# One kernel, the same operations, a new order of issue

## The chip, the core and the metric

The kernel runs on one core of a Trainium2 chip. The metric is the device time of one execution in microseconds (us). The core has five engines with a queue each: PE (matrix products; "PEld" in the profile is its weight load), DVE (element-wise work), ACT (activations and copies out of PSUM), POOL (small element-wise work, accumulating DMAs) and SP (here it only issues DMAs). An engine takes its instructions in the order in which the program lists them; it waits at the head of its queue until the semaphores of that instruction are set, and all that stands behind waits with it. 16 DMA engines carry the transfers that SP, ACT and POOL issue.

## The reference

Two blocks follow each other. The first is attention with a polynomial sketch as its kernel: for 4 batches, 4 heads, 1088 positions and 32 channels,

```python
def phi(x):
    a = np.einsum('rd,bhsd->bhsr', S1, x)
    b = np.einsum('rd,bhsd->bhsr', S2, x)
    return np.einsum('bhsi,bhsj->bhsij', a, b).reshape(*x.shape[:-1], r * r)
q_p, k_p = (phi(q), phi(k))
kv = np.einsum('bhsf,bhsd->bhfd', k_p, v)
z = np.sum(k_p, axis=2)
num = np.einsum('bhsf,bhfd->bhsd', q_p, kv)
den = np.einsum('bhsf,bhf->bhs', q_p, z)[..., None] + 1e-06
```

and its result is num / den. The heads are then joined to x of 4 x 1088 x 128, and the second block mixes along the positions:

```python
theta = x @ w_theta
zr, zi = x * np.cos(theta), x * np.sin(theta)
y = np.einsum('ts,bsd->btd', w_tok_r, zr) + np.einsum('ts,bsd->btd', w_tok_i, zi)
u = x + y
out = u + np.maximum(u @ w_ch, 0.0)
```

The two mixing matrices are 1088 x 1088 of 64-bit floats; they are most of what is read (17 blocks of 128 x 1088 words of 8 bytes, 1088 KB each), and their product with the z values is most of the arithmetic.

## The kernel before

**Operations.** The body never issues anything directly. It calls op(engine, duration, function, writes, reads, ...) some 1020 times, and each call makes a numbered operation (0 to 1019), of one to some forty instructions of one engine: "P" for PE, "V" for DVE, "A" for ACT, "G" for POOL, "S" for SP. The number counts the calls in the order of the program text.

**Order.** At the end, Layout.run takes the operations in the order that the tuple ORDER lists, and Layout.issue emits them. STARTS holds a start in hundredths of a microsecond for each place of ORDER, from a search that was run beforehand. These starts are used for two things only: which buffer of a class an operation's tile gets (a slot that is free at that start), and how many idle matmuls (`fill`, line 428) are put into gaps of PE. The durations given to op, and lk, are inputs of that search; what is emitted does not read lk, and durations enter only through those two uses.

**What the operations do, in rough order.**

- Loads. k, q and v of each batch are 576 KB each (line 671, line 668 for k of batches 0 and 1, which ACT issues). k of batches 1 to 3 is loaded twice; the second copy (line 714, "kh") is the target of an accumulating DMA that POOL issues (line 393, `big<-hf`). q of batch 3 comes in blocks turned on the way: four operations (37 to 40) of four DMAs each, line 663, 36 KB in runs of 128 bytes. The row blocks of the two matrices are "row 0" to "row 16" (line 642, `zs<-w_tok`).
- Each row block is converted from 64-bit words: two ACT operations (lines 643 and 645) into two `big` buffers, then two DVE operations. The raw block sits in one of five `zs` buffers, and the buffer is free again after the two ACT operations.
- Attention for batch 0, then 1, 2 and 3: sums over the keys ("sums", "rest"), features of k ("kT", "kf", "kv"), the chain of small scale factors ("chain"), q slices ("qT", "q0"), "levels", "den", "num", then "theta".
- Mixing. For batch 0 and batch 1 all 17 row blocks are multiplied with z and summed in PSUM ("mix"); batches 2 and 3 share seven half-size products in Winograd's scheme ("m1" to "m7"). All these matmuls are at line 399. "out" adds x, multiplies by w_ch and stores (line 1299).

**Transfers and their semaphores.** The framework gives every transfer that SP or ACT issues one of eight completion semaphores, in turn. A transfer that reuses a semaphore waits, at the head of the issuing queue, until the transfer eight places before it has landed.

**What the change touches.** ORDER and STARTS (lines 34 on), and one line of `finish` (line 1325), which gives the search a smaller duration and lk for one store operation.

## Time and profile before

| | us |
|---|---|
| median of three timed runs | 217.78 |
| these runs | 218.26, 217.74, 217.78 |
| the profiled execution, its own time | 217.81 |
| its span, first to last instruction | 215.9 |
| around the span | 1.9 |

The profile page is of that one execution. It gives each engine's busy time, the span cut in 40 slices of 5.4 us, the DMA queues, the chain of work that ended last, and the costliest groups of instructions. Views of the same trace give busy times in chosen stretches, the waits, and the instructions of one queue in order of time. PE's records are pipelined: a matmul's record is longer than the time from it to the next one, so that a busy PE shows no gap where the next matmul comes only a little late.

### The profile page before, as it was taken

What the parts mean: (1) busy time and instruction counts of PE and PEld (TensorE: products, weight loads), DVE (VectorE), ACT (ScalarE), POOL (GpSimd) and SP (SyncE); (2) the same over time, 40 slices, a digit from 0 to 9 for tenths busy, and PEclk for the clock granted to TensorE, in tenths of its full rate; (3) what the DMA queues carried; (4) which work ended last, traced back from release to release, by engine and by line L of the source; (5) the groups of instructions that cost most, each with busy time, mean ns of one, the idle gap of its engine ahead of it and who ended that gap; (6) DMA issues with size and microseconds to landing.
All of it is one profiled execution on the core that took longest, in us unless ns stands there. A gap on an engine that the chain in (4) does not pass through costs nothing.

```text
span 215.9 us, 5832 instructions
## 1 busy us (share of the span) xinstructions
PE 208.9 (97%) x2396; PEld 152.8 (71%) x2396; DVE 174.3 (81%) x343; ACT 114.5 (53%) x256; POOL 59.7 (28%) x105
## 2 busy tenths in 40 slices
PE   7899999999999999999999999999999999999992
PEld 7677798868866666866668666667677776666781
DVE  1799998999999998999999798885994747456263
ACT  4899989999998895798704233363810000000000
POOL 1272740306400000604004100000006489950403
PEclk9999999999999999999999999999999999999998
DMA  6999999995998993192002402424050420010735
GB/s 222 395 418 419 384 365 420 425 315 97 360 285 267 416 432 145 75 308 45 0 0 32 74 3 112 114 109 112 2 88 15 67 39 0 0 23 8 125 55 103
DMA packets 28046, 37.09 MB, mean 172 GB/s; under 512 B 20564, under 2 KB 23044, under 8 KB 25844
## 3 DMA queue, kind: packets, MB, share of 16 engines
q1 hardware_dynamic: 22868, 31.86, 42.4%
q0 software_dynamic: 1552, 3.25, 7.2%
q10 hardware_dynamic: 3600, 1.62, 2.8%
q8 instruction: 19, 0.31, 0.6%
q14 instruction: 7, 0.06, 0.1%
HBM read 29.84 MB, written 4.00 MB: 157 GB/s over the span
## 4 chain that ended last, share of the span: by engine, by line
PE 63%; DMA 18%; ACT 14%; issue 2%; SPq 1%; DVE 1%; POOL 1%; POOLq 0%; ACTq 0%
PE ps L399 61%; DMA zs<-w_tok 13%; DMA big<-k_l 5%; ACT big L645 4%; ACT big L643 3%; ACT lv L1056 1%; PE ps L1131 1%; ACT big L1021 1%; ACT g L1199 1%; ACT g L1202 1%; ACT g L1205 1%; ACT g L1203 1%; POOL out L1299 1%; SPq L671 0%; ACT g L1135 0%
## 5 line engine op out<-in xcount | busy, mean ns | idle before, releaser
L399 PE MATMUL ps<-big,zs 128*128 128x384 f32 (+2 forms) x380 | 110.5, 436 | 0.0
L399 PEld LDWEIGHTS ps<-big,zs 128*128 128x128 f32 x380 | 66.9, 190 | 32.5
L379 POOL TENSOR_TENSOR big<-big,big 128x544 f32<-128x544 f32 x16 | 22.1, 1458 | 48.6 <-DVE big L379 44.6
L399 PE MATMUL ps<-big,big 128*32 128x32 f32 (+2 forms) x352 | 22.8, 234 | 0.0
L643 ACT ACTIVATE big<-zs 128x1088 f32<-128x1088 f32 x17 | 20.9, 1231 | 1.5 <-DMA zs<-w_tok 0.9
L379 DVE CUSTOM_DVE_ANT_0 big<-big,big 128x2176 uint16<-128x2176 uint16 x17 | 21.5, 1275 | 0.0
L645 ACT ACTIVATE big<-zs 128x1088 int32<-128x1088 uint32 (+1 forms) x18 | 21.4, 1194 | 0.3 <-DMA zs<-w_tok 0.3
L1338 ACT COPY big<-ps 80x256 f32<-80x256 f32 x1 | 0.4, 368 | 39.6 <-DMA out<-g 39.6
L399 PEld LDWEIGHTS ps<-big,big 128*32 128x32 f32 (+1 forms) x352 | 15.3, 124 | 6.8 <-issue 0.8
L1276 ACT COPY g<-ps 128x384 f32<-128x384 f32 (+1 forms) x6 | 2.5, 466 | 23.4 <-PE ps L399 23.4
L379 DVE TENSOR_TENSOR big<-big 128x544 f32<-128x544 f32 x8 | 9.5, 1204 | 5.6 <-PE ps L399 5.6
L383 DVE TENSOR_SCALAR big<-big 128x1088 int32<-128x1088 int32 x17 | 12.2, 719 | 0.0
L379 POOL TENSOR_TENSOR mf<-mv,sm 128x32 f32<-128x32 f16 (+1 forms) x3 | 0.8, 262 | 39.1 <-DVE sm L379 39.1
L428 PE MATMUL ps<-idle 128*128 128x112 bf16 (+1 forms) x67 | 10.0, 312 | 1.3 <-POOL idle L430 1.3
L379 DVE TENSOR_TENSOR g<-lv 128x768 f32<-128x768 f32 x12 | 11.1, 950 | 0.1
L399 PEld LDWEIGHTS ps<-w,big 128*128 128x128 f32 (+1 forms) x76 | 9.8, 189 | 1.4
L379 DVE TENSOR_TENSOR big<-big,hf 128x1152 f32<-128x1152 f32 x8 | 10.7, 1351 | 0.0
L399 PE MATMUL ps<-w,big 128*128 128x128 f32 (+1 forms) x76 | 10.5, 278 | 0.0
L399 PE MATMUL ps<-sbk,g 128*128 128x64 f32 x72 | 10.0, 276 | 0.3 <-ACT g L793 0.3
L379 DVE TENSOR_TENSOR zs<-zs,g 128x384 f32<-128x384 f32 (+2 forms) x24 | 9.8, 447 | 0.2
L386 DVE SCALAR_TENSOR_TENSOR big<-ps,even,big 128x384 f32<-128x384 f32 (+1 forms) x10 | 4.8, 493 | 6.3 <-PE ps L399 6.2
L1199 ACT ACTIVATE g<-ps 128x384 f32<-128x384 f32 x12 | 5.9, 504 | 7.3 <-PE ps L399 7.3
(199 smaller groups left out, 379.2 us busy)
## 6 DMA issues: line engine op xcount, KB each, us to landing
zs<-w_tok SPq DMA_DIRECT2D x17, 1088.0 KB, 10.6
big<-k_l SPq DMA_DIRECT2D x5, 576.0 KB, 13.2
big<-v_l SPq DMA_DIRECT2D x4, 576.0 KB, 15.6
big<-q_l SPq DMA_DIRECT2D x3, 576.0 KB, 10.7
big<-hf POOLq DMA_DIRECT2D x3, 576.0 KB, 10.0
far<-zs SPq DMA_DIRECT2D x3, 576.0 KB, 2.8
zs<-far SPq DMA_DIRECT2D x12, 144.0 KB, 4.3
big<-k_l ACTq DMA_DIRECT2D x2, 576.0 KB, 4.4
```

Of the source, the lines that this page charges most:

```text
L379: eng.tensor_tensor(out=o, in0=a, in1=b, op=f)
L383: (eng or V).tensor_scalar(out=o, in0=a, scalar1=s1, scalar2=s2, op0=op0, **kw)
L386: (eng or V).scalar_tensor_tensor(out=o, in0=a, scalar=s, in1=b, op0=op0, op1=op1)
L399: T.matmul(o, lhs, rhs, start=start, stop=stop, skip_group_check=True)
L428: T.matmul(nowhere()[:, :n], idle()[:, 0:P], idle()[:, :n], start=True, stop=True, skip_group_check=True)
L643: op("A", 0.22 + n * 0.0009, lambda: A.activation(dfn(), words_of(raw(), n)[1].bitcast(F32), AF.Prelu, scale=2.0**-112, alpha=-(2.0**32)), ...
L645: op("A", 0.22 + n * 0.0009, lambda: A.activation(stp(), words_of(raw(), n)[0].bitcast(U32), AF.Copy, scale=2.0**-29), [stp], [raw])
L1021: op("A", act(GW) + 0.1, lambda g=g, tr=tr: A.activation(f()[:, g * GW:(g + 1) * GW], tr(), AF.Copy, scale=s()[:, 0:1]), [(f, g)], [tr, (s ...
L1056: op("A", act(480), lambda g=g, lp=lp: A.copy(lv().rearrange("p l (c n) -> p l c n", n=HR)[:, :, g * GC:(g + 1) * GC], lp().rearrange("p c ...
L1131: T.transpose(tr()[:, i * P:(i + 1) * P], qp()[:, i * H + 2 * n:i * H + 2 * n + 2].rearrange("p h i j -> p (h i j)"), ident())
L1199: op("A", act(GW), lambda cs=cs, th=th: A.activation(cs()[:, 0], th(), AF.Copy, bias=ROUND), [(cs, 0)], [th])
L1276: op("A", act(w), lambda: A.copy(u(), yp()[:, :w]), [uT], [yp])
```

## The change

The operations and their code are the same. ORDER lists them in another order, and STARTS has other starts. Of the 412 PE operations 47 keep their place in PE's queue, of DVE's 266 also 47, of ACT's 237 it is 45, of POOL's 53 it is 23 and of SP's 52 it is 16. The idle matmuls of 384 columns go from 28 to 26. The order of the transfers, up to the last row block, is as follows (k2 is k of batch 2, kh its second copy, q3a to q3d the four operations 40, 38, 37 and 39; the ACT queue issues k0 and k1):

```
before: k0 k1 k3 q0 row1 k2 w2 q2 row3 kh1 v0 row8 q1 row2 v1 row0 v3 kh3 row7 row5 row4 kh2
        q3d q3c row6 v2 row9 q3a q3b row10 row13 row11 row15 row14 row12 row16
after:  k0 k1 k3 row1 k2 q0 w2 row3 q2 q1 kh1 v0 row2 row0 v2 q3a q3b v3 v1 kh3 row7 row6 row4
        kh2 row9 row5 row8 q3c q3d row12 row10 row11 row13 row14 row15 row16
```

In the last 20 places of ORDER no engine's own order changes. The one line of code:

```diff
@@ finish, line 1325
         elif b and t0 < 2 * GW:
-            op("S", w * P * 4 / 100e3, lambda: (store(SY, 0, 2), store(G, 2, 4)), [], [ot], due, lk=4)
+            op("S", w * P * 2 / 100e3, lambda: (store(SY, 0, 2), store(G, 2, 4)), [], [ot], due, lk=2)
```

and the tables, cut to their first line each:

```diff
 ORDER = (
-    29, 32, 4, 2, 5, 0, 1, 3, 34, 30, 356, 50, 33, 102, 44, 96, 6, 108, 103, 36, 7, 51, 366, 54, 144, 8, 97, 10, 9,
...
+    29, 4, 2, 5, 32, 0, 1, 3, 34, 356, 33, 30, 44, 50, 366, 36, 96, 35, 6, 54, 51, 102, 139, 7, 108, 144, 10, 55, 97,
...
 STARTS = (
-    73, 73, 90, 92, 103, 130, 170, 220, 358, 404, 449, 458, 493, 510, 538, 546, 566, 579, 580, 584, 594, 612, 628,
...
+    73, 90, 92, 103, 115, 130, 170, 220, 234, 278, 324, 368, 414, 458, 458, 504, 510, 598, 566, 579, 580, 596, 602,
...
```

## The prediction

> **What bounds the kernel now.** I read the page's busy times first, then busy times by stretch, then the chain that ended last, then SP's queue. From the page:

> ```profile
> PE 208.9 (97%) x2396; PEld 152.8 (71%) x2396; DVE 174.3 (81%) x343; ACT 114.5 (53%) x256; POOL 59.7 (28%) x105
> DMA  6999999995998993192002402424050420010735
> GB/s 222 395 418 419 384 365 420 425 315 97 360 285 267 416 432 145 75 308 45 0 0 32 74 3 112 114 109 112 2 88 15 67 39 0 0 23 8 125 55 103
> ```

> PE has 7.0 us without a record in 215.9. The DMA engines are full up to about 82 us (slice 15) but for slices 9 and 12, and hardly used later. Busy times by stretch (PE, PEld, DVE, ACT, POOL, then PE's granted clock, DMA share, GB/s):

> ```profile
> 0.00:15.00 15.00, 12.70 (x216) 10.92 (x217) 8.59 (x39) 10.89 (x28) 5.27 (x23) 1.00 0.88 337
> 15.00:30.00 15.00, 14.71 (x278) 11.62 (x276) 14.59 (x35) 14.21 (x38) 6.34 (x16) 1.00 1.02 389
> 30.00:45.00 15.00, 14.63 (x325) 13.25 (x326) 14.20 (x30) 14.30 (x38) 3.93 (x13) 1.00 1.02 414
> 45.00:60.00 15.00, 15.00 (x292) 11.62 (x292) 14.76 (x27) 14.40 (x31) 6.06 (x12) 1.00 0.85 245
> 60.00:78.00 18.00, 18.00 (x246) 12.14 (x248) 17.82 (x29) 16.38 (x25) 0.00 (x0) 1.00 0.97 340
> 140.00:210.00 70.00, 70.00 (x298) 48.78 (x297) 44.26 (x85) 11.03 (x24) 26.84 (x23) 1.00 0.25 49
> ```

> From 45 us on PE shows no gap. Before that four things are nearly full at once (DMA, DVE, ACT, PE), so the order decides how soon PE has all the work it can take; what PE loses there is lost at the end. From 140 on the columns alone set the pace: 83,712 columns in 70 us, 0.84 ns each; between 94 and 114 it is 24,576 in 20 us, 0.81. The chain, where DMA hands over to PE:

> ```profile
> 3.63 11.58 DMA big<-k_l
> 15.22 16.38 DMA zs<-w_tok
> ...
> 66.30 10.64 DMA zs<-w_tok
> 77.02 1.27 ACT big L645
> 78.29 0.09 ACT sm L850
> 78.42 3.41 PE ps L399 x55
> ```

> The first two lines show the eight semaphores: k2 lands at 15.21, and row 2, eight transfers on, is issued at 15.22. The last four show a late row block (row 11, landing at 76.94) in front of ACT; the copy behind it (L850) then lets PE go on. SP's queue and ACT's at that place:

> ```profile
> 37.11 14.49 SPq L663 DMA_DIRECT2D big<-q_l  x8
> ...
> 53.25 11.66 SPq L663 DMA_DIRECT2D big<-q_l  x8
> 65.02 12.05 SPq L642 DMA_DIRECT2D zs<-w_tok  x6
> ```

> ```profile
> 74.38 1.22 ACT L643 ACTIVATE big<-zs 128x1088 f32<-128x1088 f32 x1 [0.29 <-DMA zs<-w_tok]
> ...
> 77.02 1.27 ACT L645 ACTIVATE big<-zs 128x1088 int32<-128x1088 uint32 x1 [0.31 <-DMA zs<-w_tok]
> ```

> q3's sixteen short-row pieces hold SP for 26.15 us, and rows 10, 13 and 11 stand behind the second eight.

> **The change, part by part.** The sum is made against the profiled 217.81, 0.03 over the median.

> *Line 1325 and the idle matmuls: 0.* The line changes what the search is told, nothing that is issued. Two idle matmuls fewer fill time in which PE waits anyway; with PEclk at 1.00 in every stretch up to 210 no clock is at stake. Cover gone, two cost at most 0.6 (mean record 0.31).

> *How I place things.* ACT is 95% busy from 15 to 60 us, so its work ahead of an operation tells when it gets there. I add the trace's durations of all ACT operations ahead of it in the new list, and look up when ACT in the old run had done as much. Landings go by spacing in SP's queue: q2 to row 3 17.38 to 19.97, 2.59 a row block; row 3 to kh1 19.97 to 21.36, 1.39 a 576 KB tensor. An accumulating DMA (10.0 us from issue to landing) slows the rest: from kh1 (21.36) the four transfers up to row 2 need 7.96 by that spacing, and row 2 came at 31.60, 2.3 late. The page's slice 8, with another one in it, shows 315 GB/s after 425: 1.4 of its 5.4 us. So one costs 1.4 to 2.3.

> *Late rows: minus 0.3.* Rows 12, 10, 11 and 13 now follow the last eight pieces. Row 12's raw buffer is row 5's, which ACT frees at about 62.9; the fastest row landing is 5.5 us after issue, so 68.4, and ACT gets there (64.6 us of work) at 70.0. Row 10: 71.0 against 72.7. Row 11: 73.6 against 80.9. The two waits shown, 0.29 and 0.31, go, and PE's stall behind them. PE's loss is between 0.05 (its gap in 78 to 84) and 0.6 (both waits); I take the middle.

> [...]

> *q3's first eight pieces ahead of v3: plus 0.1.* The new list carries the same bytes up to v2 as the old one up to v1, which landed at 32.99 (row 2 at 31.60 plus 1.39). The eighth piece reuses v2's semaphore, so SP is held until 33.0, and v3, v1, kh3, row 7 and all later ones are issued after 33.65, where before v3, kh3, row 7 and row 5 were issued between 19.97 and 27.66. The DMA engines run empty and start anew: v3 lands at 36.5 (the 2.8 us of `far<-zs`, also 576 KB) to 38.0 (row's 5.5 less 1.2). Three tensors and six rows more (19.7 us), one accumulating DMA (1.4 to 2.3), then 0 to 1.4 of a second: row 8 lands at 57.6 to 61.4. ACT gets to it (54.6 us of work ahead; 23.9 before) at 59.4. Behind it in ACT's queue stand chain's, row 5's and theta's operations, for which DVE and then PE wait. It is 0 to 2.0 late; ACT's own idle time in 60 to 78 is 1.62, which takes most of it up. Row 7 lands at 41.9 to 43.4 against 42.5, row 4 at 48.5 to 50.9 against 49.7: the same picture, 0 to 1.2. kh3 lands at 39.3 to 40.8; its accumulating DMA, issued by POOL at 39.89 before, is at most 1 later, and has 16 us until PE's sums read the result (56.3), of which it needs 10. Middles meet; 0.1 for the upper half.

> *First 20 us: plus 0.1.* Row 1 and k2 go ahead of q0. ACT gets to k3 at 8.6 (landed 8.2), to row 1 at 10.7 (10.8), to k2 at 13.2 (12.2 to 13.8), to q0 at 14.5. Before k2 landed at 15.21 with the same bytes ahead as q0 has now, so ACT waits up to 0.7 there; before it needed q0 only at 11.8, landed by then. ACT has 0.79 idle in 15 to 30 and 0.70 in 30 to 45 to make it good: 0 to 0.7.

> *DVE's and POOL's own order: 0.* DVE does the same work up to row 8 and is as full as ACT (14.59, 14.20 and 14.76 of 15). What moves on it moves with the ACT results that it reads, priced above; for a wait of its own I bound both signs by its idle time in 30 to 45, 0.8. POOL is idle for over half of every stretch; its first accumulating DMA waits for kh1, now behind q1: 1.4 later, landing near 33 where PE read it at 34.2 before. 0, with the same bound.

> *After 84 us: 0.* PE has no gap, and the DMA share is a quarter. Moved stores (batch 0's go from 155 to 185, batch 1's from 200 to 184) and POOL's joins for batch 1, now earlier, end long before the tail, which is unchanged. Bounds 0 and 0.5, the latter if a turned x comes late once.

> Sum: 217.81 - 0.3 + 0.1 + 0.1 = 217.7.

> **The rivals.**

> *Faster: all of ACT's idle time in 60 to 78 was PE's loss.* For it: SP is late there, and the chain runs through it. Against it: PE shows no gap there. At 1.0 of the 1.62: 216.8.

> *Slower: the train of loads behind 33.65.* One place, ACT's first conversion of row 8. It decides from a landing of row 8 after 61.0 (59.4 plus 1.62): each us more is one us for PE. At 62.2, if the accumulating DMAs cost 2.3 each and the restart is slow: 219.0. For it: the DMA engines are full in the whole stretch, and before issued its v3 13.7 us sooner. Against it: ACT reaches row 8 later than 59.4 if it has waited earlier.

> *Slower: the first 20 us.* q0 later than 15.2 holds ACT by more than it can make good, with PE at 12.70 of 15 and everything else queued behind: 0.8, 218.6.

> **How the numbers follow.** 0.3% is 0.65 us, about what a measurement of this kernel can tell from no change. The sum's own case, within 217.1 to 218.4: 0.46. Faster rival 0.23, row 8 0.18, first 20 us 0.13, so slower 0.31. 216.8 is the faster rival's time and leaves perhaps 0.1 below; 219.0 leaves 0.1 above.

> **What would show it.** Right: no ACT wait on `zs<-w_tok` between 70 and 80; SP's first v load after the short pieces at 33 to 34, and a hole in the DMA's slices there; ACT's wait at row 8 under 1.6 us; PE without a gap after 45 us. Wrong: a long ACT wait on `zs<-w_tok` near 60, or on `big<-q_l` near 15, with PE gaps behind it; or PE gaps after 84, for which I have no cause.

## The result, and the profile after

The changed kernel takes 221.52 us (median of six runs, 221.32 to 223.56) against 217.98 for the kernel before (217.74 to 218.26): a ratio of 1.017, with a 95% interval of 1.0144 to 1.0195. It is 3.5 us slower, and outside the range 216.8 to 219.0. The profiled execution took 221.48, with a span of 219.7. Ratios and intervals below leave disturbed runs out and medians do not, so that the two can differ, by 1.8 us in c3 and by some tenths elsewhere.

The page of the kernel after, its busy times by stretch (PE, PEld, DVE, ACT, POOL, then PE's granted clock, DMA share, GB/s), and SP's queue in order of time:

```profile
PE 210.0 (96%) x2394; PEld 152.8 (70%) x2394; DVE 173.4 (79%) x343; ACT 114.7 (52%) x256; POOL 55.8 (25%) x105
DMA  6999996999973998094002120424271100300275
GB/s 225 394 416 421 399 247 215 403 333 385 402 194 102 383 404 339 11 329 89 0 0 39 30 39 3 145 74 157 62 111 26 30 3 0 72 0 0 52 120 100
```

```profile
15.00:30.00 15.00, 13.99 (x274) 11.53 (x278) 13.90 (x32) 12.81 (x37) 7.19 (x22) 1.00 1.02 393
30.00:45.00 15.00, 14.07 (x342) 12.62 (x330) 14.72 (x33) 14.05 (x37) 3.98 (x13) 1.00 0.86 295
45.00:60.00 15.00, 14.43 (x285) 11.86 (x285) 13.61 (x24) 13.48 (x30) 6.24 (x12) 1.00 1.02 367
60.00:78.00 18.00, 17.51 (x167) 10.89 (x166) 15.58 (x27) 14.94 (x25) 0.00 (x0) 1.00 0.75 242
140.00:210.00 70.00, 69.63 (x354) 48.15 (x353) 43.37 (x87) 12.70 (x30) 26.05 (x23) 1.00 0.25 53
```

```profile
18.31 15.60 SPq L663 DMA_DIRECT2D big<-q_l  x8
34.04 1.03 SPq L671 DMA_DIRECT2D big<-v_l  x2
...
50.42 15.40 SPq L663 DMA_DIRECT2D big<-q_l  x8
68.63 0.33 SPq L642 DMA_DIRECT2D zs<-w_tok  x1
```

The hole is where it was foreseen: SP is held from 18.3 to 33.9, and two slices of 5.5 us move 247 and 215 GB/s. But PE now has more gaps in all stretches from 15 to 78 us, and one behind 140. The chain that ended last shows two kinds of them before 78 us:

```profile
16.09 0.24 PE ps L399
16.33 0.48 issue
16.82 0.27 PE ps L399
...
41.55 0.28 PE ps L1018 x2
41.82 0.75 issue
42.57 0.27 PE ps L1018
...
50.04 15.21 DMA zs<-w_tok
65.25 0.02 issue
65.27 1.21 ACT big L643
```

The last three lines are row 8. It is issued at 50.04 and lands at 65.25; the prediction had it landing at 57.6 to 61.4 and ACT there at 59.4. Row 4 landed at 52.6 (said: 48.5 to 50.9). Row 8 was issued only when ACT had freed the raw buffer that it goes into, a wait that the prediction does not have; four transfers from row 4 to row 5 were then still on their way, so it is not shown that this wait made the landing later. ACT's waits between 20 and 84 us begin with these two rows (total, number of waits, longest):

```profile
ACT big L643 <- DMA zs<-w_tok: 3.7, 2, 2.6
```

The other gaps, 0.48 and 0.75, stand against "issue": PE waits there for nothing that the profile names. With a third one, 0.23 at 63.4, they come to 1.5 us.

### The profile page after: what moved, and what is told of

Same layout as the page of the kernel before. It is cut to its first block, busy times and chain, and to the rows that moved or that the text cites. A ratio compares the mean times of both kernels' runs of the same rounds, so it can differ in the third digit from the quotient of the medians.

```text
span 219.7 us, 5825 instructions
## 1 busy us (share of the span) xinstructions
PE 210.0 (96%) x2394; PEld 152.8 (70%) x2394; DVE 173.4 (79%) x343; ACT 114.7 (52%) x256; POOL 55.8 (25%) x105
## 3 DMA queue, kind: packets, MB, share of 16 engines
q10 hardware_dynamic: 3600, 1.62, 2.7%
## 4 chain that ended last, share of the span: by engine, by line
PE 69%; DMA 11%; ACT 6%; DVE 6%; POOL 5%; issue 3%; SPq 0%; POOLq 0%; ACTq 0%
PE ps L399 64%; DMA zs<-w_tok 11%; POOL big L379 3%; PE ps L1131 2%; ACT big L645 2%; PE ps L1018 2%; DVE big L379 1%; POOL out L1299 1%; ACT big L643 1%; PE ps L428 1%; DVE sm L379 1%; DVE big L383 1%; ACT big L693 1%; ACT big L991 1%; PE ps L790 0%
## 5 line engine op out<-in xcount | busy, mean ns | idle before, releaser
L399 PE MATMUL ps<-big,zs 128*128 128x384 f32 (+2 forms) x380 | 111.1, 437 | 0.7 <-POOL big L379 0.4
L399 PEld LDWEIGHTS ps<-big,zs 128*128 128x128 f32 x380 | 66.7, 190 | 35.3 <-POOL big L379 1.0
L379 POOL TENSOR_TENSOR big<-big,big 128x544 f32<-128x544 f32 x16 | 21.3, 1394 | 12.4 <-PE ps L399 10.3
L643 ACT ACTIVATE big<-zs 128x1088 f32<-128x1088 f32 x17 | 20.8, 1222 | 6.0 <-DMA zs<-w_tok 4.2
L399 PE MATMUL ps<-big,big 128*32 128x32 f32 (+2 forms) x352 | 22.2, 234 | 0.2 <-ACT g L743 0.2
L393 POOL DMA_DIRECT2D g<-big x6 | 5.2, 875 | 63.7 <-ACT g L1276 63.7
L645 ACT ACTIVATE big<-zs 128x1088 int32<-128x1088 uint32 (+1 forms) x18 | 21.2, 1185 | 0.3 <-DMA zs<-w_tok 0.3
L399 PEld LDWEIGHTS ps<-big,big 128*32 128x32 f32 (+1 forms) x352 | 14.7, 124 | 4.8 <-ACT g L743 0.5
L399 PEld LDWEIGHTS ps<-w,big 128*128 128x128 f32 (+1 forms) x76 | 9.9, 189 | 2.9 <-ACT big L1144 0.8
L399 PE MATMUL ps<-w,big 128*128 128x128 f32 (+1 forms) x76 | 10.9, 280 | 0.6 <-ACT big L1144 0.6
L379 DVE TENSOR_TENSOR big<-big,hf 128x1152 f32<-128x1152 f32 x8 | 10.8, 1348 | 0.0
L379 DVE TENSOR_TENSOR big<-big,ps 128x160 f32<-128x160 f32 (+1 forms) x6 | 2.6, 434 | 10.0 <-PE ps L399 10.0
L1056 ACT COPY lv<-ps 128x480 f32<-128x480 f32 x12 | 6.4, 559 | 7.9 <-PE ps L399 7.8
L399 PE MATMUL ps<-sbk,g 128*128 128x64 f32 x72 | 10.2, 278 | 0.2 <-ACT kg L701 0.2
L399 PEld LDWEIGHTS ps<-sbk,g 128*128 128x128 f32 x72 | 9.0, 191 | 1.8 <-issue 0.9
```

The costliest lines, as they stand in the source:

```text
L379: eng.tensor_tensor(out=o, in0=a, in1=b, op=f)
L393: op("G", 0.9, lambda: G.dma_start(dst(), src(), accum_op=ALU.add), w, r, fly=fly)
L399: T.matmul(o, lhs, rhs, start=start, stop=stop, skip_group_check=True)
L643: op("A", 0.22 + n * 0.0009, lambda: A.activation(dfn(), words_of(raw(), n)[1].bitcast(F32), AF.Prelu, scale=2.0**-112, alpha=-(2.0**32)), ...
L645: op("A", 0.22 + n * 0.0009, lambda: A.activation(stp(), words_of(raw(), n)[0].bitcast(U32), AF.Copy, scale=2.0**-29), [stp], [raw])
L1056: op("A", act(480), lambda g=g, lp=lp: A.copy(lv().rearrange("p l (c n) -> p l c n", n=HR)[:, :, g * GC:(g + 1) * GC], lp().rearrange("p c ...
```

## The experiments

Where an operation is moved, a few lines at the end of `run` do it, after the buffers have been chosen, so that no other operation moves; (40, 215) puts operation 40 behind operation 215.

```diff
+MOVES = ((40, 215), (38, 40))
...
+        for i, j in MOVES:
+            o = self.order.pop(self.order.index(self.ops[i]))
+            self.order.insert(self.order.index(self.ops[j]) + 1, o)
```

| run | base, edit | median, us | ratio to before, 95% |
|---|---|---|---|
| a1 | after, first eight pieces behind kh2 | 221.05 | 1.0151 (1.0097 to 1.0206) |
| a2 | after, rows 8 and 9 change places (and buffers) | 221.13 | 1.0136 (1.0100 to 1.0171) |
| a3 | after, batch 1's stores behind POOL's sums | 220.93 | 1.0115 (1.0089 to 1.0141) |
| b1 | before, last eight pieces ahead of v3 | 225.13 | 1.0298 (1.0250 to 1.0346) |
| c1 | after, 59 short idle matmuls for 39 | 231.26 | no ratio (four runs, 227.7 to 231.8) |
| c2 | a1 + a3 + 30 idle matmuls | 219.60 | 1.0056 (1.0026 to 1.0085) |
| c3 | before, 59 short idle matmuls for 39 | 224.65 | 1.0221 (1.0133 to 1.0309) |
| c4 | after, 30 idle matmuls for 39 | 221.20 | 1.0154 (1.0104 to 1.0204) |
| d1 | a1 + 30 idle matmuls | 219.99 | 1.0078 (1.0050 to 1.0107) |
| d2 | c2 with 32 idle matmuls | 219.27 | 1.0055 (1.0031 to 1.0079) |
| d3 | before, 30 idle matmuls for 39 | 217.61 | 0.9980 (0.9951 to 1.0010) |

**a1: is it the train of loads?** My first theory was the slower rival of the prediction with a larger size: SP's hold makes rows 4 and 8 late, and ACT's waits there are the loss. The edit is the diff above.

> The changed kernel (221.5) with q3's first eight pieces (operations 40 and 38) moved in the list from ahead of v3 to behind kh2; buffers and all other places as in the changed kernel. Train theory: the pieces hold SP until v2 has landed and leave the DMA engines half empty around 27 to 38 us, so that row 4 and row 8 land late in front of ACT. SP then issues v3 ten us earlier, the two slices of 247 and 215 GB/s fill up, row 4 lands before ACT gets there (50.7), and 2.0 to 3.1 us come back: 218.4 to 219.5. Order theory: the loss lies in the new order of DVE, ACT and POOL, and ACT's waits for rows only replace others: 221.1 to 221.9.

It came out at 221.05. SP was free (first line: v2, v3 and v1 are issued by 26.2, before the pieces), row 4 landed at 45.4, seven us sooner, and PE was 1.4 us ahead of the kernel after at batch 3's key sums (55.95 against 57.34). By 63.5 it had lost all of that. SP's queue and the chain of a1:

```profile
14.27 11.89 SPq L671 DMA_DIRECT2D big<-v_l  x3
...
33.48 14.55 SPq L663 DMA_DIRECT2D big<-q_l  x8
```

```profile
61.42 0.33 PE ps L399
61.74 1.80 issue
63.54 5.32 PE ps L399 x17
```

So the step from loads to rows to ACT is real up to there, but taking it away returned 0.5 us, which the intervals cannot tell from nothing: something else stops PE at 63.5.

**a2: row 8 alone.** Rows 8 and 9 change places in the list, numbers 391 and 396.

```diff
-... 165, 448, 173, 166, 396, 200, 354, ...
+... 165, 448, 173, 166, 391, 200, 354, ...
...
-... 484, 473, 391, 471, 485, 365, 37, ...
+... 484, 473, 396, 471, 485, 365, 37, ...
```

> The changed kernel with rows 8 and 9 changing places in SP's queue and buffers (two numbers of the list): row 8 is issued at 38 and lands near 57, row 9 is issued at 50 and lands near 65. ACT converts row 8 at 60.5 if nothing holds it, row 9 near 68. Train theory: ACT's wait of 2.6 us or more at row 8 goes, the 2 us at row 4 stay; 1.0 to 1.8 us come back: 219.7 to 220.5. Order theory: 221.1 to 221.9.

221.13: nothing that can be told from the kernel after. ACT's longest wait for a row fell from 2.6 to 1.1 us, and PE stood still at the same matmul as in a1, for 0.56 us, until 63.60.

**a3: POOL's stores.** In the kernel before, batch 1's first store operation stood behind POOL's sums for Winograd's seventh product; the change put it between two of them. `MOVES = ((623, 957),)` puts it back behind.

> The changed kernel with one store operation (623, batch 1's first 384 columns, two DMAs by SP and two by POOL) moved in the list from between POOL's sums 954 and 953 to behind the last sum (957). POOL theory: POOL's two stores take 1.36 us between two sums of the chain that the seventh Winograd product waits for, and PE loses 0.5 to 0.6 us there: 220.9 to 221.1, with the first matmul of m7_0 without a gap. Rival: POOL's chain has slack, or the product waits for the next sum all the same: 221.3 to 221.7.

220.93. POOL's queue, first in the kernel before, then in the kernel after, then in a3:

```profile
181.54 10.58 POOL L379 TENSOR_TENSOR big<-big,big 128x544 f32<-128x544 f32 x8 [0.41 <-POOL big L379]
199.97 2.58 POOL L1299 DMA_DIRECT2D out<-g  x4 [7.85 <-DVE g L1303]
```

```profile
181.82 7.81 POOL L379 TENSOR_TENSOR big<-big,big 128x544 f32<-128x544 f32 x6 [1.94 <-PE ps L399]
189.57 1.35 POOL L1299 DMA_DIRECT2D out<-g  x2
190.93 6.50 POOL L379 TENSOR_TENSOR big<-big,big 128x544 f32<-128x544 f32 x5
```

```profile
181.16 14.26 POOL L379 TENSOR_TENSOR big<-big,big 128x544 f32<-128x544 f32 x11 [1.95 <-PE ps L399]
195.37 1.34 POOL L1299 DMA_DIRECT2D out<-g  x2
```

Two DMAs of 96 KB together, 1.35 us of POOL's time, stood in front of five sums. PE's gap at the first matmuls of the seventh product (0.37 at 192.33 by the records; 0.53 if it is counted, as below, from start to start over what is usual for the shape) is gone in a3: PE runs 0.66 us ahead of the kernel after just before this place and 1.30 ahead from there on, so it is worth 0.64 between these two executions.

**b1: the place of the pieces, in the order of before.** Here the moves are made before the buffers are chosen, since q3 needs its buffer sooner, and some other tiles take other buffers too: `MOVES = ((40, 351), (38, 40))`.

> The kernel before (218.0) with q3's last eight pieces (operations 40 and 38) moved up to behind row 0, so that they stand ahead of v3, kh3, row 7, row 5 and row 4, as in the changed kernel; all other work in the order of before (q3 and some others take other buffers). Train theory: SP is held until 33, row 7 and kh3 land 3 to 4 us late, ACT waits at row 7 (41) or row 4 (48); rows 10, 13 and 11 no longer stand behind pieces, which gives back up to 0.3: 219.0 to 220.5. Order theory: the place of the pieces costs nothing, and the rows come earlier: 217.5 to 218.1.

225.13, far more than either theory said. SP is held until 37.4, row 7 goes out at 38.62 and lands at 46.93 (41.13 before), and PE has nothing to do until ACT has converted it. The chain of b1, and its windows:

```profile
38.62 8.31 DMA zs<-w_tok
46.93 0.02 issue
46.96 1.17 ACT big L643
48.13 0.22 ACT big L805
48.35 0.04 issue
48.39 1.49 PE ps L399 x6
```

```profile
30.00:45.00 15.00, 14.23 (x322) 12.79 (x320) 13.95 (x30) 12.32 (x32) 3.88 (x13) 1.00 0.83 285
45.00:60.00 15.00, 11.70 (x126) 7.98 (x126) 8.47 (x18) 9.75 (x21) 4.62 (x11) 0.66 0.84 250
```

PE stood still for 3.3 us and got half its clock for 10.2 us, from 47.7 on (0.66 in the second row). So the train costs much where a row is needed at once (1.0298 in b1); in the kernel after, where the list asks for the rows later, a1 alone got 0.5 us back.

**What "issue" is.** The trace has the packets of a queue of its own, "instruction", 16 KB each; 19 of them lie in the span. Between 59 and 60.9 us of the kernel after there is none; in the next 1.05 us there is one (queue, packets, MB, share of the 16 engines):

```profile
q0 software_dynamic: 34, 0.16, 57.9%
q1 hardware_dynamic: 30, 0.19, 46.0%
q8 instruction: 1, 0.02, 5.8%
```

I put the end of each packet beside PE's next start after an "issue" gap, and counted which matmul of the program that is, from 0 and with the idle ones:

```
kernel   matmul  operation      packet          PE goes on  after its end  PE idle
after     221    79 qscale0     14.34 to 15.39  16.82       1.43           0.48
after     728    335 qT1        40.23 to 41.17  42.57       1.40           0.75
after    1108    503 mix0_0     60.95 to 61.92  63.37       1.45           0.23
a1        728    335 qT1        39.78 to 40.86  42.29       1.43           0.52
a1       1108    503 mix0_0     61.11 to 61.99  63.54       1.55           1.80
a2       1108    503 mix0_0     61.30 to 62.22  63.60       1.38           0.56
a3       1108    503 mix0_0     61.20 to 62.15  63.59       1.44           0.55
```

The matmul is the same in kernels in which PE comes to it at times 1.4 us apart, and the wait ends 1.4 to 1.6 us after the packet. 221, 728 and 1108 are 507 and 380 apart, 4 and 3 times some 127. I take the packets for PE's own program, a block of some 127 matmuls with their weight loads in each: the 19 packets stand beside 2394 matmuls, 126 a packet. That is an estimate from these counts; no view names what a packet holds. If so, PE's next block came only while PE ran the one before: counted in steps of 127 matmuls, the packets of the kernel after started 1.9 to 5.2 us after PE had entered the block before, up to 84 us. The waits come to 1.5 us in this kernel, and to 1.8 at one block of a1.

**c1: the blocks alone.** If a block's place in the program matters, idle matmuls at the very start must matter by their number, with the same columns and nearly the same time:

```diff
-    first = op("P", 3.2, lambda: [spin(112) for _ in range(39)], [nowhere], [idle], due=-10.0)
+    first = op("P", 3.2, lambda: [spin(74) for _ in range(59)], [nowhere], [idle], due=-10.0)
```

> The changed kernel (221.5) with PE's 39 idle matmuls of 112 columns at the very start cut into 59 of 74, the same columns; nothing else differs. Block theory: PE's program comes in blocks of 16 KB through the DMA engines, the next block is asked for only when PE enters the one before it, and in the changed kernel PE stands still at the matmuls number 221, 728 and 1108 because their block has landed only 1.4 us before. Twenty matmuls more in front move every block's first matmul 20 places forward in the program, where PE comes by sooner; with the waits of the blocks as they were (2.8 to 5.2 us behind the data) PE then loses 10.6 us at these places instead of 1.8: 226 to 230, PE standing still at matmul 1108 as counted again, now 20 places earlier in the list of operations. Rival: the gaps at those matmuls have another cause (a buffer or an operand) and stay at operations 79, 335 and 503: 221.1 to 222.0.

231.26 (the profiled execution took 230.88): twenty more idle matmuls, with the same columns, cost 6 to 10 us, by the run. The chain of c1:

```profile
14.94 1.26 issue
16.20 0.80 PE ps L790 x3
...
59.06 3.15 PE ps L399 x140
62.21 4.16 issue
66.37 7.08 PE ps L399 x16
```

PE stands still at matmul 221 (now an operation of k of batch 3) and at matmul 1109 by the order of the records (1108 was foreseen), now the last of batch 3's sums, some twenty matmuls sooner in the list, and goes on 1.2 us after the block's packet (64.14 to 65.16). No gap is left at operations 79, 335 or 503. PE's share in 60 to 78 us:

```profile
60.00:78.00 18.00, 13.84 (x208) 8.93 (x207) 12.22 (x16) 12.45 (x24) 1.29 (x5) 0.81 0.46 118
```

0.81 is the clock: at each of the two stops, of 3.1 and 4.2 us, a stretch of 6.8 us at half clock began, which the expectation did not have.

**c3 and d3: the kernel before.** The same edit (59 of 74), and the other way (30 of 146 columns).

> The kernel before (218.0) with its 39 idle matmuls of 112 columns at the start cut into 59 of 74. Block theory: here the blocks land 0.9 to 1.5 us ahead of PE's need; 20 matmuls more use that up at matmuls 221 and 1108 and cost 1.2 to 2.0: 219.2 to 220.0. Rival: 217.7 to 218.4.

> The kernel before with 30 idle matmuls of 146 columns at the start instead of 39 of 112. Block theory: no block holds PE there with 39, and with 9 fewer none does either (0.1 at most): 217.7 to 218.4, no gap 1.3 to 1.6 us after a block's end. Rival: the number of idle matmuls acts by itself (a colder PE, an earlier or later start), and 30 instead of 39 changes this kernel as 59 did, which cost 3 to 7 us: 220 or more, or under 217.

59 cost 1.0221, some 4.8 us and not 1.2 to 2.0. The profiled execution of c3 is the slowest of its four (225.99; the others took 221.44 to 224.99), so that its stops may be larger than those behind the ratio:

```profile
13.43 1.54 issue
...
60.32 3.16 issue
63.48 4.55 PE ps L399 x16
```

PE stands still for 1.5 us at matmul 222, for 0.4 at 727 and for 3.2 at 1108, where the block now began at 61.0 instead of 56.9. 30 cost nothing (0.998, interval across 1). So it is not the idle matmuls by themselves. The kernel before had its blocks 0.9 to 1.5 us ahead of need at 221, 728 and 1108 (PE came there 2.3 to 2.9 us after the packet's end, and I take off the 1.4 of the table), and twenty matmuls use that up.

**c4, c2, d1, d2: rows and blocks together.** c4 has `[spin(146) for _ in range(30)]` and nothing else, d1 that and the move of a1, c2 the move of a3 as well, d2 is c2 with `[spin(137) for _ in range(32)]`.

> The changed kernel with 30 idle matmuls of 146 columns at the start instead of 39 of 112, and nothing else. Block theory: the gaps at matmuls 221 and 1108 (operations 79 and 503) go, a gap of 1.2 us opens at matmul 348 (operation 77, rest0), 0.3 stays at 728: the loss at blocks is 1.4 instead of 1.8: 220.8 to 221.5. Rival: gaps stay at operations 79, 335 and 503: 221.3 to 221.9.

> The changed kernel with the first eight pieces behind kh2 (the run a1, 221.05), batch 1's stores behind POOL's sums (the run a3, 220.93) and 30 idle matmuls of 146 columns at the start instead of 39 of 112. Block theory: in the run a1 the rows no longer held PE, but block 1108 did (1.96 us); 9 matmuls less move it to where PE comes by later, and of the 2.6 us lost at blocks 1.1 are left (at matmul 348): 218.6 to 219.4. Rival: blocks have no part, and the two moves just add up: 220.2 to 220.7.

> The changed kernel with the first eight pieces behind kh2 (the run a1) and 30 idle matmuls of 146 columns at the start (the run c4); the stores stay. Two limits in a row (late rows at 50 to 57 us, late blocks of PE's program at 16, 42 and 63 us): each alone hides the gain of taking the other away, and both away give 1.5 to 2.2 us, to 219.2 to 220.0, with POOL's gap of 0.5 at the first matmuls of m7 left. Rival: the gains of a1 (0.5) and c4 (0.3) add: 220.5 to 221.0.

> As the run c2 (219.6), with 32 idle matmuls of 137 columns instead of 30 of 146. Block theory: the gap of 0.48 us at matmul 348 (operation 77) shrinks to 0.2 or less, and block 1108 still comes in time: 0.2 to 0.4 less than c2. It is at the time of the kernel before, not under it: 218.0 to 219.3.

c4 has no gap at operations 79, 335 and 503 any more (the one of 1.2 us foreseen at matmul 348 came out at 0.2), and still takes 221.2: with the blocks in time, ACT's waits for rows are what is left (from c4, 20 to 84 us),

```profile
ACT big L643 <- DMA zs<-w_tok: 4.1, 3, 1.9
```

and PE's gap at 55.3, behind row 4, grew from 0.7 to 1.1. d1 takes both away: between 20 and 84 us it shows no "issue" gap of PE over 0.2 us and no wait of ACT for a row, and

```profile
60.00:78.00 18.00, 18.00 (x234) 11.98 (x236) 17.71 (x31) 16.51 (x28) 0.00 (x0) 1.00 0.81 274
```

It stands at 1.0078, while a1 and c4 alone stand at 1.0151 and 1.0154, and their gains of 0.2% each would add up to 1.0135. So two limits follow each other; together they are 0.9%, 2.0 us. That each hides what the other one is worth is what the traces suggest (a1 lost its 1.4 us at a block, c4 still waits for rows); by the times alone the intervals of a1 and c4, half a per cent to either side, are too wide to rule out that the gains just add up. c2, with the stores too, stands at 1.0056 (median 219.60, expected 218.6 to 219.4), and PE's stretches of c2 from 45 to 78 us are again close to those of before:

```profile
45.00:60.00 15.00, 14.93 (x284) 12.07 (x284) 14.76 (x25) 14.25 (x31) 6.82 (x12) 1.00 0.98 293
60.00:78.00 18.00, 17.88 (x234) 11.85 (x236) 16.59 (x30) 15.98 (x27) 0.00 (x0) 1.00 0.81 261
```

d2 was to shrink the gap at operation 77 to 0.2; it stayed at 0.45, and the time at 1.0055. That block landed 0.3 us later than in c2 (22.34 against 22.06), and PE had waited 0.3 us at the block before it as well.

## Why the prediction was wrong

What the runs account for, of 3.7 us by the ratio 1.017: 2.0 for late rows and late blocks together (d1), 0.6 for POOL's stores (a3), and 1.2 that c2 still has over the kernel before (0.6 to 1.9 by its interval). How the 2.0 divides between rows and blocks stays open, since neither a1 nor c4 returned more than 0.5.

**The step that failed** is not one of the terms but one that the sum lacks: PE's program. "Line 1325 and the idle matmuls: 0" priced two idle matmuls by the time they fill and the clock they hold, and the whole working took PE's instructions as being there. In the kernel before the blocks landed 0.9 to 1.5 us early at matmuls 221, 728 and 1108, so no view showed a wait; the new order used that up three times, and PE stood still for 0.48, 0.75 and 0.23 us.

**"Q3's first eight pieces ahead of v3: plus 0.1"** had the mechanism right and two sizes wrong. SP was held until 33.9 (said: 33.65), and the hole is there. But kh3 landed at 42.3 (39.3 to 40.8), row 7 at 44.7 (41.9 to 43.4), row 4 at 52.6 (48.5 to 50.9) and row 8 at 65.25 (57.6 to 61.4). The spacing of 2.59 us a row block was read where rows follow each other in full; row 8 is followed at once by the second eight pieces and shares its last ten us with an accumulating DMA (54.57 to 64.83); the slice from 60.4 to 65.9 moves 194 GB/s. No run took pieces and accumulating DMA apart. The rival that named ACT's first conversion of row 8 had the place; "each us more is one us for PE" was wrong: ACT's 2.6 us there are worth little by themselves, as a2 shows, since PE was held elsewhere too. Taken at its word, this rival gives 222.0 for the landing at 65.25, and that this is near 221.5 is luck.

**"Late rows: minus 0.3".** ACT was to wait for no row between 70 and 80 us; it still does, for row 10:

```profile
77.59 1.21 ACT L645 ACTIVATE big<-zs 128x1088 int32<-128x1088 uint32 x1 [0.26 <-DMA zs<-w_tok]
```

That it is the only one between 70 and 80 us is because ACT comes later: row 12 landed at 73.6, not 68.4, and ACT was to be there at 70.0. The pieces held SP until 65.8, and the raw buffer for row 12 came free at 68.6 (said: 62.9), when ACT had got past the late row 8. Nothing was gained that the runs could show.

**"After 84 us: 0 (0 to 0.5)"** looked at when moved stores end, and not at what stands behind them on the queue that issues them: 1.35 us of POOL's time in the one chain that PE waits for there, 0.64 us.

**"First 20 us: plus 0.1"** was right where it looked: q0 landed at 13.5, and ACT got there at 14.6 without a wait. **"DVE's and POOL's own order: 0 (±0.8)"** may hold a part of c2's remaining 1.2 us. Counted from start to start over what is usual for the same shape, most of what c2 loses against the kernel before lies ahead of 45 us, and its largest gaps there are 0.6 at 15.35 (a result of DVE, by the waits), 0.4 at 16.3 (one of ACT, behind q0's conversion) and 0.5 at a block at 23.5, which is PE's program again. No run took these apart, and the cause of this part stays open.

## What to carry to other kernels

Where PE shows an "issue" gap, look at the packets of the instruction queue: where one had ended 1.2 to 1.6 us before PE went on, I read it here as PE waiting for its program, and twenty matmuls more ahead of such places cost some 5 (c3) and 6 to 10 us (c1). In this kernel the waits stood where some 127 matmuls took 5 to 6 us while the DMA engines were full of data (a DMA share of 1.02 to 1.13 as the three packets came); the slack that the old kernel has there belongs into the sum, like that of a buffer. And where two limits follow each other, as here, take them away together before you call either one harmless.
